# Turning x on TensorE in float32 instead of by the DMA queue, and re-ordering the experts' products and rows, in an attention and two-MoE kernel on one core

## The chip, the core and the metric

The kernel runs on one core of a Trainium2 chip. The core's engines run side by side: TensorE (PE in the profile; PEld is its weight loading), VectorE (DVE), ScalarE (ACT), GpSimd (POOL) and SyncE (SP), which here does nothing but issue DMAs. ACT issues some DMAs as well. Each engine takes its instructions in program order, and waits between engines are semaphores. The metric is the device time of one execution in microseconds, the median of several runs.

## The reference

Three stages follow one another; the output of one is the input of the next.

```python
# attention: batch 4, 8 heads, 576 rows, head size 64
scores = scale * q @ k.T                         # per batch and head
scores = where(scores >= max(scores) - tau, scores, -1e9)
attn = exp(scores - max(scores)); attn /= attn.sum() + 1e-9
x = (attn @ v), heads side by side               # 2304 x 512
# first MoE: one expert, d_ff 2048
h = x @ w_in;  g = maximum(0.01 * h, h);  x = g @ w_out
# second MoE: 8 experts of 4 slots each, hidden 1024
logits = x @ phi                                 # 2304 x 32
slot_input = softmax_over_tokens(logits).T @ x   # 32 x 512
slot_out[e] = maximum(slot_input[e] @ w1[e], 0) @ w2[e]
out = softmax_over_slots(logits) @ slot_out      # 2304 x 512
```

## The kernel before

The 2304 tokens are cut into 18 tiles of 128. Float32 accuracy in the large products is kept by splitting an operand into two 16-bit words, a high one and a low one (`value - high`), and adding three products.

**The order of the work** is not written by hand. `emit` describes operations (`Plan.add`: engine or alternative engines, priority, planned duration, buffers read and written), and `Plan.schedule` places them greedily by planned times; its result is the program order of every engine. So a change of one operation moves others, too. PSUM has few buffers: "S" (2) for the scores, "X" (1) for the attention output, "h" (2) for the first MoE's products, "misc" (1) for all small things.

**One tile in the main loop.** `attention(t)` makes the scores (L1089), the row maximum (DVE L1102), the exponential (ACT L1123), the threshold (DVE L1130), the high word (ACT L1156) and the low words (POOL L1166), turns the probabilities by DMA (SP L1188, two transposing DMAs for a pair of heads) and multiplies with v into X (PE L1198). Then x is X divided by the row sums (DVE L1220), its high word (ACT L1228), its low word (L1231, on DVE or POOL as the plan decides), and a transposing DMA of eight 128x128 blocks into the tile `xT` (SP L1238). `feed(t, xT, xh)` multiplies xT with w_in: 48 matmuls of 512 columns (PE L1266) in four groups j of twelve, each into one "h" buffer, which ACT empties (L1279, L1285); the low word of r (L1288, POOL or DVE) and a transposing DMA (SP L1311) follow, and the logits (PE L1321, L1325). `block` folds two tiles into the running slot sums (PE L1494). Beside the first tiles w_in and w_out are converted from 64-bit words, and w_out is stored to a scratch tensor.

**The tail** comes after the last tile. The slot sums are turned (L1647), multiplied with w_out, which is loaded back (L1659, four accumulating groups c side by side in the four 32-column strips of TensorE), and turned again (L1672). Then come the experts. `load` (L1690) brings in 64 pieces of w1 and 64 of w2, each 256 KB in a buffer of the pool of tags `CH`, as buffers of the main loop come free. The w1 products (L1702) run for expert group G (4 experts), half n of the hidden columns, expert j, and innermost the four pieces k of the contraction; expert j writes strip 32j to 32j+31 of the output. So four matmuls in a row accumulate in one strip:

```python
for j in range(4):
    e = 4 * G + j
    for k in range(4):
        w = load(a["w1"][e, k * P : (k + 1) * P, n * 512 : (n + 1) * 512], T0 - 7)
```

The results are turned (L1715) for the w2 products (L1773), two matmuls of 256 columns for each piece, and the output is made in two halves of 256 columns: one matmul for each tile (L1802), emptied by ACT or DVE (L1809, L1812), stored for two tiles at a time (L1820). A piece of w2 is read, and the output written, as two runs of 256 floats (1 KB) on a partition. Stores of the first half are issued behind the last load.

Of the kernel before, what the change touches and what calls it, by code (L numbers as in the profile page):

```python
# [9 lines left out]
F32 = mybir.dt.float32  # L10
# [10 lines left out]
P = 128  # L21
# [320 lines left out]
def emit(tc, a, out, dbg=None, opt=None):  # L342
# [4 lines left out]
    O = dict(  # L347
        LH=2.3, LB=2.6, HG=3, NR=13, NT=6, NW=5, XH=1, XT=4, KX=10, VX=5, AE=2, AH=3, AT=3, QH=2, QL=2,
        QR=2, TQ=("qr", "raw"), KR=2, VR=4, RAW=1, G=2, PO=0.3, PI=-8.0, PV=-3.0, DA=-100, TK=("kr",
        "w2"), TV=("vr", "kr"), TX=("kx", "w2"), TH=(0, 2), VP=1, MT=0, PS=0.15, NM=6, E=1, LA=2, MG=0,  # L350
        MH=0, RES=0, MI=(2, 1, 2, 1), MO=(1, 1, 1, 1), WT=("w",), PST=0, BH=1, DP={"vr": 1.0, "xT":
        0.1, "xh": 0.25, "X": -0.25, "kx": -1.0, "x32": 0.1, "g": 0.25, "E": -0.1, "S": -1.0, "h": 1.0,
        "r": 1.0, "rT": 0.5, "qr": 1.0, "ql": 0.25, "qh": 1.0, "ah": 0.5, "vx": -0.1, "misc": -1.0,
        "dh": -0.25, "kr": -0.25, "z": -0.1, "th": 0.5, "aT": -1.0}, LO=4, LP=2, PB=1, TU=("x32", "xh",
        "xT", "rT"), TO=("raw", "rT"), TE=18, TR=18, TG=("g",), BI={"spa": 300}, LG=0, CAP=(("aT",
        1),), PL=-0.5, TL=("rT", "xT", "ae"), NA=24, QU=(), CT=0, CX=("aT",), TW=("aT", "ql", "qh",
# [368 lines left out]
    for k in range(4):  # L725
        w32, pk = floats_of(PW, a["w_in"], k, (S23, ("x32", "rT", "xh", "xT"), "raw_in"))
# [410 lines left out]
    def attention(t):  # L1137
# [5 lines left out]
        for pr in range(4):  # L1143
# [40 lines left out]
            for i in range(2):  # L1184
# [571 lines left out]
    HC, firsts = DM // 2, []  # L1756
    outv = out.rearrange("(t i p) d -> t p i d", i=2, p=P)
    so_ps = pl.buf("X", [P, 2, HC])
    for hf in range(2):
        pt = T0 + 2 + hf  # L1760
        cols = slice(hf * HC, hf * HC + HC)
# [34 lines left out]
        for t in range(0, NTILE, 2):  # L1796
# [8 lines left out]
            for i in range(2):  # L1805
# [29 lines left out]
def host(inputs):  # L1835
# [10 lines left out]
    va = np.concatenate([vf, np.concatenate([vl, vl], axis=2)], axis=3)  # L1846

    def bits(w):
        return np.ascontiguousarray(np.asarray(w)).view(np.int64)
# [24 lines left out]
```

## Time and profile before

| | |
|---|---|
| median of 3 runs | 666.04 us (664.19 to 670.23) |
| the profiled execution | 668.88 us, of which 667.1 us are the span of the profile |
| busy share of the span | PE 79%, DVE 66%, ACT 64%, POOL 52% |
| DMA queue of SP | 90.3% of 16 engines' span |
| matrix clock granted, mean | 0.934 |
| instructions | 15257 |

The profile is one execution. Its span starts with the first instruction. Stages can be told by the lines that run in them: conversions until about 115 us, the steady loop until about 537 us, the last tile's products until 566 us, then the tail. [...] Matmul durations overlap each other, so the distance between starts, not the duration, says what a matmul costs. A float32 matmul shows as two records, one for each pass.

### The profile page before, as it was taken

To read this page: it belongs to the slowest core of one execution; us is meant where nothing else is said; L and a number is where in the kernel's file an instruction comes from. 1 tells how busy PE (TensorE), PEld (TensorE's weight loads), DVE (VectorE), ACT (ScalarE), POOL (GpSimd) and SP (SyncE) were. 2 spreads that over 40 slices of the span, in tenths; PEclk is the share of its full clock that TensorE was granted. 3 is DMA by queue.
4 is the path that set the end of the run, shared out by engine and by line. 5 is a ranking of instruction groups with operands and counts; after the bars stand their busy time and mean duration, and the time that the engine had idled before them with its cause. 6 is when DMAs were issued, how large, how long until landed. Compare 5 with 4: busy or idle time off the path is not lost. (4 is left out here: it accounts for less than half of the span.)

```text
span 667.1 us, 15257 instructions
## 1 busy us (share of the span) xinstructions
PE 527.1 (79%) x5622; PEld 322.4 (48%) x5622; DVE 442.1 (66%) x1068; ACT 425.9 (64%) x806; POOL 345.9 (52%) x364
## 2 busy tenths in 40 slices
PE   0111787989799988889799989898979696499994
PEld 0011576666466545555465556565545453132553
DVE  6999978888678767878686976577776531201033
ACT  7999778776587776889677867575765542111022
POOL 3553445575676676868657877676774600000000
PEclk9999967989899999999699999799999897789998
DMA  8954889998999999999989999999998999899995
GB/s 304 338 212 123 201 227 217 249 198 183 168 192 236 190 172 186 178 211 213 182 162 189 189 155 192 207 186 168 171 156 144 256 224 242 283 381 348 365 311 196
DMA packets 316522, 145.26 MB, mean 218 GB/s; under 512 B 270624, under 2 KB 291616, under 8 KB 316448
## 3 DMA queue, kind: packets, MB, share of 16 engines
q1 hardware_dynamic: 309248, 130.56, 90.3%
q10 hardware_dynamic: 7200, 13.73, 8.3%
q8 instruction: 44, 0.72, 0.5%
q14 instruction: 30, 0.25, 0.1%
HBM read 69.27 MB, written 8.91 MB: 117 GB/s over the span
## 5 line engine op out<-in xcount | busy, mean ns | idle before, releaser
L1166 POOL TENSOR_TENSOR ah<-ae,ah 128x512 f16<-128x512 f32 (+1 forms) x216 | 206.4, 978 | 97.4 <-ACT ah L1156 72.2
L1266 PE MATMUL h<-wh,xT 128*128 128x512 f16 x864 | 217.4, 391 | 10.0 <-DMA xT<-xh 9.8
L1102 DVE TENSOR_REDUCE nm<-S 128x1 f32<-128x576 f32 x144 | 103.0, 748 | 62.7 <-PE S L1089 62.7
L1123 ACT ACTIVATE ae<-S,nm 128x576 f32<-128x576 f32 x144 | 100.8, 738 | 40.6 <-DVE nm L1102 32.9
L1266 PEld LDWEIGHTS <-xT 128*128 128x128 f16 x864 | 77.6, 101 | 91.3 <-issue 12.7
L1130 DVE SCALAR_TENSOR_TENSOR ae<-S,th,ae 128x576 f32<-128x576 f32 x144 | 113.7, 812 | 11.1 <-ACT ae L1123 10.3
L1198 PE MATMUL X<-vx,aT 128*128 128x64 f16 (+1 forms) x2240 | 94.2, 200 | 30.0 <-DMA aT<-ah 29.9
L1198 PEld LDWEIGHTS <-aT 128*128 128x128 f16 (+1 forms) x2240 | 82.4, 105 | 62.8 <-DMA aT<-ah 41.7
L1156 ACT ACTIVATE ah<-ae 128x576 f16<-128x576 f32 x144 | 96.0, 681 | 10.5 <-DVE ae L1130 8.9
L1089 PE MATMUL S<-kx,qh 64*128 64x288 f32 (+1 forms) x600 | 82.4, 340 | 6.8 <-DVE ae L1130 6.2
L1279 ACT ACTIVATE g<-h 128x512 f32<-128x512 f32 x72 | 42.9, 596 | 49.5 <-PE h L1266 42.7
L1089 PEld LDWEIGHTS S<-kx,qh 64*128 64x128 f32 (+1 forms) x600 | 56.0, 199 | 25.9 <-issue 21.5
L1288 POOL TENSOR_TENSOR r<-g,r 128x512 f16<-128x512 f32 x42 | 48.8, 1166 | 17.1 <-ACT r L1285 17.1
L1089 PE MATMUL S<-kx,ql 64*128 64x288 f32 (+1 forms) x280 | 48.3, 316 | 11.2 <-DVE ql L975 11.2
L1285 ACT ACTIVATE r<-g 128x512 f16<-128x512 f32 x72 | 45.0, 628 | 0.4
L1288 DVE TENSOR_TENSOR r<-g,r 128x512 f16<-128x512 f32 x30 | 28.9, 965 | 20.1 <-ACT r L1285 20.1
L1089 PEld LDWEIGHTS S<-kx,ql 64*128 64x128 f32 (+1 forms) x280 | 32.3, 202 | 11.6 <-DVE ql L975 11.6
L496 PE MATMUL misc<-c,tmp 128*1 128x128 f32 x16 | 4.5, 380 | 33.4 <-DVE tmp L563 30.0
L1321 PE MATMUL misc<-c,rT 128*128 128x64 f16 x288 | 19.0, 190 | 9.5 <-DMA rT<-r 9.5
L1321 PEld LDWEIGHTS <-rT 128*128 128x128 f16 x288 | 17.5, 97 | 12.2 <-DMA rT<-r 10.0
L799 PE MATMUL misc<-c,w 128*128 128x32 f32 x128 | 19.3, 298 | 4.4 <-DVE w L791 2.6
L1231 POOL TENSOR_TENSOR xh<-x,xh 128x512 f16<-128x512 f32 x12 | 14.4, 1200 | 15.3 <-ACT xh L1228 12.6
(334 smaller groups left out, 828.8 us busy)
## 6 DMA issues: line engine op xcount, KB each, us to landing
wh<-in_w SPq DMA_DIRECT2D x29, 256.0 KB, 6.4
r<-in_w SPq DMA_DIRECT2D x24, 256.0 KB, 5.2
rT<-in_w_out SPq DMA_DIRECT2D x22, 256.0 KB, 3.5
ah<-in_w_in SPq DMA_DIRECT2D x9, 512.0 KB, 5.9
kx<-in_w SPq DMA_DIRECT2D x16, 256.0 KB, 5.9
ae<-in_w_in SPq DMA_DIRECT2D x7, 512.0 KB, 4.3
vr<-in_v SPq DMA_DIRECT2D x10, 320.0 KB, 4.1
scr<-w SPq DMA_DIRECT2D x12, 256.0 KB, 3.9
```

Source lines behind the costliest of these rows:

```text
L1089: pe.matmul(out=pss[i].ap[:rows, n, :HALF], lhsT=l.ap[64 * i : 64 * i + 64, pr, :rows], rhs=m.ap[64 * i : 64 * i + 64, n * HALF : (n + 1) ...
L1102: lambda: dve.tensor_reduce(out=nm.ap, in_=ps.ap[:, :, :HALF], axis=AX.XY, op=ALU.max, negate=True),
L1123: lambda: act.activation(out=e(), in_=ps.ap[:, :, :HALF], func=AF.Exp, bias=nm.ap[:, 0:1], scale=1.0),
L1130: lambda: dve.scalar_tensor_tensor(out=e(), in0=ps.ap[:, :, :HALF], scalar=th.ap[:, 0:1], in1=e(), op0=ALU.is_ge, op1=ALU.mult, accum_out= ...
L1156: (lambda ah, ae, i: lambda: act.activation(out=ah.ap[:, i, :S], in_=ae.ap[:, i], func=AF.Copy))(ah, ae, i),
L1166: (lambda ah, ae: lambda: pool.tensor_tensor(out=ah.ap[:, h, w0 : w0 + c1 - c0], in0=ae.ap[:, h, c0:c1], in1=ah.ap[:, h, c0:c1], op=ALU.su ...
L1198: pe.matmul(out=X.ap[r0:r1, 2 * pr + i], lhsT=aT.ap[:, c, r0:r1], rhs=vtiles[b, pr].ap[:, wv, cv], start=(pr == 0 and i == 0 and n == 0), ...
L1266: pe.matmul(out=hp.ap, lhsT=xT.ap[:, wx * 4 + k], rhs=wh[k][j].ap[:, ww], start=(n == 0), stop=(n == 11),)
L1279: (lambda g, hp: lambda: act.activation(out=g.ap, in_=hp.ap, func=AF.Prelu, alpha=0.01))(g, hp),
L1285: (lambda j, g: lambda: act.activation(out=r[j].ap[:, 0], in_=g.ap, func=AF.Copy))(j, g),
L1288: fg = lambda eng, j, g: lambda: eng.tensor_tensor(out=r[j].ap[:, 1], in0=g.ap, in1=r[j].ap[:, 0], op=ALU.subtract)
L1321: pe.matmul(out=L.ap, lhsT=rT[j].ap[:, c], rhs=wq.ap[:, 4 * j + c], start=(j == 0 and c == 0), stop=False,)
```

## The change

Four things change. (1) x is turned by four float32 transposes on PE (L1229 of the new code) into an "h" buffer of PSUM, out of which ACT writes the high word of `xT` (L1233) and DVE the low word (L1238, always DVE). The ACT copy and the subtraction in front of the DMA, the tile `xh`, and the transposing DMA go. `x32` has two buffers now. (2) The w1 loop has the expert j innermost. (3) The host stores w2 such that a piece is one run of 2 KB on each partition. (4) The output tensor has a layout in which a store writes one run of 2 KB for each partition; the host puts it in order afterwards.

```diff
-        xh, xT = pl.buf("xh", [P, 2, DM], F16), pl.buf("xT", [P, 8, P], F16)
+        xp, xT = pl.buf(O["XP"], [P, 4, P], F32, "xp"), pl.buf("xT", [P, 8, P], F16)
+
+        def f():
+            for k in range(4):
+                pe.transpose(xp.ap[:, k], x32.ap[:, k * P : (k + 1) * P], ident.ap)
+
+        pe_op(p, 440, f, r=[x32, ident], w=[xp])
         act_op(
-            p, t_act(512), lambda: act.activation(out=xh.ap[:, 0], in_=x32.ap, func=AF.Copy),
-            r=[x32], w=[(xh, 0)],
-        )
-        fx = lambda eng: lambda: eng.tensor_tensor(
-            out=xh.ap[:, 1], in0=x32.ap, in1=xh.ap[:, 0], op=ALU.subtract
-        )
-        add_alt(p, [("dve", P2(t_dve(512)), fx(dve)), ("pool", t_pool(512), fx(pool))], r=[x32, (xh, 0)], w=[(xh, 1)])
-        att_last.append(
-            dma_t(
-                p, 8,
-                lambda: sp.dma_start_transpose(out=xT.ap, in_=xh.ap.rearrange("p a b -> p (a b)")),
-                r=[xh], w=[xT],
-            )
+            p, 490, lambda: act.activation(out=xT.ap[:, 0:4], in_=xp.ap, func=AF.Copy), r=[xp],
+            w=[(xT, 0)],
+        )
+        dve_op(
+            p, 602,
+            lambda: dve.tensor_tensor(
+                out=xT.ap[:, 4:8], in0=xp.ap, in1=xT.ap[:, 0:4], op=ALU.subtract
+            ),
+            r=[xp, (xT, 0)], w=[(xT, 1)],
         )
...
-            for j in range(4):
-                e = 4 * G + j
-                for k in range(4):
+            for k in range(4):
+                for j in range(4):
+                    e = 4 * G + j
                     w = load(a["w1"][e, k * P : (k + 1) * P, n * 512 : (n + 1) * 512], T0 - 7)
...
                     w = load(
-                        a["w2"][4 * G + j, c * P : (c + 2) * P, cols].rearrange("(k p) d -> p k d", p=P),
-                        T0 - 7, [P, 2, HC],
+                        a["w2"][hf, 4 * G + j, c // 2].rearrange("p (k d) -> p k d", k=2), T0 - 7, [P, 2, HC]
                     )
...
-                (lambda t, ot, cols: lambda dq: dq.dma_start(
-                    out=outv[t // 2, :, :, cols], in_=ot.ap))(t, ot, cols),
+                (lambda t, ot, hf: lambda dq: dq.dma_start(
+                    out=out[hf, t // 2], in_=ot.ap.rearrange("p i d -> p (i d)")))(t, ot, hf),
```

Lines behind L1073 have other numbers in the new code: 2 less in the attention, 1 more in `feed` and in the tail's w1 part. The next rows are ACT's order around the x of the twelfth tile, before. `x` is the float32 tile, `xh` its two words, `ah` the probabilities' words, `dh` a small tile of `block`.

```order
L1123 ACTIVATE ae<-S,nm 128x576 x2
L1401 ACTIVATE sm<-sm 128x1
L1409 ACTIVATE E,sm<-misc,sm 128x256
L1228 ACTIVATE xh<-x_6282 128x512
L1156 ACTIVATE ah<-ae 128x576
```

And ACT's order at the same tile now; `g` and `r` (L1280, L1286) are the emptying of an "h" buffer of the tile before.

```order
L1121 ACTIVATE ae<-S,nm 128x576 x2
L1280 ACTIVATE g<-h 128x512
L1286 ACTIVATE r<-g 128x512
L1233 ACTIVATE xT<-h 128x512
L1154 ACTIVATE ah<-ae 128x576 x2
```

ACT's part of x stood behind two exponentials and the work of `block`; it now stands behind the emptying of the last product of the tile before, and reads PSUM. The next rows are PE's order at the same place now: the last matmul of the tile before, the four transposes, twelve score matmuls, and the first of fourteen X matmuls of the next tile (L1196); the first matmul that reads the new `xT` follows those fourteen.

```order
L1267 MATMUL h<-wh,xT 128x512
L1229 MATMUL h<-c_78,x_6370 128x128 x4
L1087 MATMUL S<-kx,qh 128x288 x4
L1087 MATMUL S<-kx,ql 128x288 x2
L1087 MATMUL S<-kx,qh 128x288 x4
L1087 MATMUL S<-kx,ql 128x288 x2
L1196 LDWEIGHTS aT
L1196 MATMUL X<-vx,aT 128x64
```

Before, PE had no instruction between X and the first product of a tile that belonged to x. The last piece is DVE's order there now: x (L1218), thresholds, two selections of the next tile's scores (L1128), the low word of `xT`.

```order
L1218 TENSOR_TENSOR x_6370<-X,rz 128x512
L1107 TENSOR_SCALAR th<-nm,c_101 128x1
L1128 SCALAR_TENSOR_TENSOR ae,z<-S,th,ae 128x576 x2
L1238 TENSOR_TENSOR xT<-h,xT 128x512
L1100 TENSOR_REDUCE nm<-S 128x1 x2
```

The low word stood on POOL for 12 of the 18 tiles before; it stands on DVE behind two selections now.

## Rows read from the trace of the kernel before

**Rows 1.** Busy time by stage: stretch, length, engines (instructions), PEclk, DMA share, GB/s

```profile
115.00:537.00 422.00, 373.27 (x4528) 236.08 (x4528) 315.06 (x755) 301.79 (x562) 291.38 (x306) 0.96 1.06 190
...
537.00:566.00 29.00, 24.36 (x158) 10.95 (x158) 8.52 (x17) 10.30 (x22) 0.50 (x1) 0.88 1.07 241
...
588.50:627.40 38.90, 38.59 (x153) 11.96 (x154) 3.50 (x7) 5.14 (x9) 0.00 (x0) 0.96 1.08 362
...
654.50:667.10 12.60, 3.89 (x20) 2.76 (x20) 5.40 (x13) 3.33 (x8) 0.00 (x0) 0.74 0.57 188
```

**Rows 2.** The x transposing DMA (L1238): durations of issue, first and last start, who waited

```profile
L1238 SPq DMA_TRANSPOSE xT<-xh x18: 1231/1252/3459, 112.9 to 541.1; - x18
...
  PE h L1266: 9.8, 6
```

**Rows 3.** Timeline of the twelfth and thirteenth tiles: start, us, engine, line, [idle before]

```profile
387.84 0.68 DVE L1220 TENSOR_TENSOR x<-X,rz 128x512 f32<-128x512 f32 x1
...
391.79 1.23 SPq L1238 DMA_TRANSPOSE xT<-xh  x1
...
395.05 1.47 PE L1266 MATMUL h<-wh,xT 128*128 128x512 f16 x6 [1.02 <-DMA xT<-xh]
...
422.81 1.46 PE L1266 MATMUL h<-wh,xT 128*128 128x512 f16 x3 [3.31 <-DMA xT<-xh]
```

**Rows 4.** Busy time in a stretch behind the longest of these waits

```profile
421.50:428.40 6.90, 5.59 (x30) 3.27 (x30) 2.23 (x4) 1.08 (x3) 4.16 (x5) 0.51 1.19 244
```

**Rows 5.** Groups by line: busy us, mean ns of one, idle before and releaser

```profile
L1198 PE MATMUL X<-vx,aT 128*128 128x64 f16 (+1 forms) x2240 | 94.2, 200 | 30.0 <-DMA aT<-ah 29.9
...
L1231 POOL TENSOR_TENSOR xh<-x,xh 128x512 f16<-128x512 f32 x12 | 14.4, 1200 | 15.3 <-ACT xh L1228 12.6 <-issue 1.8 <-DMA aT<-ah 0.8
...
L789 ACT ACTIVATE w<-h 128x512 f32<-128x512 f32 x9 | 5.4, 598 | 5.6 <-PE h L783 5.6
L791 DVE COPY w<-h 128x512 f32<-128x512 f32 x7 | 4.8, 688 | 3.3 <-PE h L783 3.2
```

**Rows 6.** PE timeline: groups of four float32 transposes, at full and at low clock

```profile
588.81 1.09 PE L1745 MATMUL misc<-c,qr 128*96 128x128 f32 x4 [0.44 <-DVE aT L1679]
...
631.94 0.60 PE L1715 MATMUL h<-c,qh 128*128 128x128 f32 x4
```

**Rows 7.** Chain of waits: the last X matmuls of the last tile; then its products' records

```profile
537.08 0.58 PE X L1198 x14
...
L1266 PE MATMUL h<-wh,xT x864: 376/379/634, 116.3 to 565.8; 128*128 128x512 f16 x173
```

**Rows 8.** PE timeline: w_out products with four strips in turn, then w1 products

```profile
585.39 0.59 PE L1659 MATMUL h<-raw,aT 128*32 128x512 f32 x1
...
585.41 0.59 PE L1659 MATMUL h<-vx,aT 128*32 128x512 f32 x1
585.82 0.59 PE L1659 MATMUL h<-raw,aT 128*32 128x512 f32 x1
...
600.16 0.62 PE L1702 MATMUL S<-xT,aT 128*32 128x512 f32 x1
600.17 0.62 PE L1702 MATMUL S<-x,aT 128*32 128x512 f32 x1
600.61 0.59 PE L1702 MATMUL S<-xT,aT 128*32 128x512 f32 x1
```

**Rows 9.** SP's timeline: issue of the first and of the last w2 load

```profile
593.59 0.38 SPq L1690 DMA_DIRECT2D kr<-in_w  x1
...
640.49 0.37 SPq L1690 DMA_DIRECT2D kr<-in_w  x1
```

**Rows 10.** DMA packets from 577 to 594 us (w1), and from 600 to 620 us (w2)

```profile
DMA packets 3631, 6.64 MB, mean 390 GB/s; under 512 B 404, under 2 KB 404, under 8 KB 3628
...
DMA packets 7213, 6.97 MB, mean 349 GB/s; under 512 B 421, under 2 KB 7212, under 8 KB 7212
```

**Rows 11.** DMA issues: KB each, median us from issue to landing

```profile
r<-in_w SPq DMA_DIRECT2D x24, 256.0 KB, 5.2
```

More of the change, by code (lines that the diff above doesn't have):

```diff
@@ L347, in emit @@
     O = dict(
-        LH=2.3, LB=2.6, HG=3, NR=13, NT=6, NW=5, XH=1, XT=4, KX=10, VX=5, AE=2, AH=3, AT=3, QH=2, QL=2,
+        LH=2.3, LB=2.6, HG=3, NR=13, NT=6, NW=5, NX=2, XT=4, KX=10, VX=5, AE=2, AH=3, AT=3, QH=2, QL=2,
         QR=2, TQ=("qr", "raw"), KR=2, VR=4, RAW=1, G=2, PO=0.3, PI=-8.0, PV=-3.0, DA=-100, TK=("kr",
-        "w2"), TV=("vr", "kr"), TX=("kx", "w2"), TH=(0, 2), VP=1, MT=0, PS=0.15, NM=6, E=1, LA=2, MG=0,
+        "w2"), TV=("vr", "kr"), TX=("kx", "w2"), TH=(0, 2), VP=1, MT=0, PS=0.15, NM=6, E=1, LA=2, XP=("h",), MG=0,
         MH=0, RES=0, MI=(2, 1, 2, 1), MO=(1, 1, 1, 1), WT=("w",), PST=0, BH=1, DP={"vr": 1.0, "xT":
@@ L353, in emit @@
         "r": 1.0, "rT": 0.5, "qr": 1.0, "ql": 0.25, "qh": 1.0, "ah": 0.5, "vx": -0.1, "misc": -1.0,
-        "dh": -0.25, "kr": -0.25, "z": -0.1, "th": 0.5, "aT": -1.0}, LO=4, LP=2, PB=1, TU=("x32", "xh",
-        "xT", "rT"), TO=("raw", "rT"), TE=18, TR=18, TG=("g",), BI={"spa": 300}, LG=0, CAP=(("aT",
+        "dh": -0.25, "kr": -0.25, "z": -0.1, "th": 0.5, "aT": -1.0}, LO=4, LP=2, PB=1, TU=("x32", "xT",
+        "rT"), TO=("raw", "rT"), TE=18, TR=18, TG=("g",), BI={"spa": 300}, LG=0, CAP=(("aT",
         1),), PL=-0.5, TL=("rT", "xT", "ae"), NA=24, QU=(), CT=0, CX=("aT",), TW=("aT", "ql", "qh",
@@ L413, in emit @@
         ("r", "main", O["NR"]), ("rT", "main", O["NT"]), ("w", "main", O["NW"]),
-        ("x32", "main", 1), ("xh", "main", O["XH"]), ("xT", "main", O["XT"]),
+        ("x32", "main", O["NX"]), ("xT", "main", O["XT"]),
         ("qr", "main", O["QR"]), ("qh", "main", O["QH"]), ("ql", "main", O["QL"]), ("kr", "main", O["KR"]),
@@ L568, in floats_of @@
         return ws, pow2_of(prio, hw)
-    pl.early.update(("raw_in", "raw_out"))
+    pl.early.update(("raw_in", "raw_out", "xp"))
     if O["WT"] != ("w",):
@@ L725, in emit @@
     for k in range(4):
-        w32, pk = floats_of(PW, a["w_in"], k, (S23, ("x32", "rT", "xh", "xT"), "raw_in"))
+        w32, pk = floats_of(PW, a["w_in"], k, (S23, ("x32", "rT", "xT"), "raw_in"))
         sk = scale_from(PW + 0.16, pk, 4.0)
@@ L1071, in split_v @@
         vtiles[b, pr] = vx
-    att_last = []
     def scores(t, pr, prio, qs):
@@ L1225, in attention @@
         )
-        xh, xT = pl.buf("xh", [P, 2, DM], F16), pl.buf("xT", [P, 8, P], F16)
+        xp, xT = pl.buf(O["XP"], [P, 4, P], F32, "xp"), pl.buf("xT", [P, 8, P], F16)
[3 more added lines that the diff above has]
+        pe_op(p, 440, f, r=[x32, ident], w=[xp])
         act_op(
-            p, t_act(512), lambda: act.activation(out=xh.ap[:, 0], in_=x32.ap, func=AF.Copy),
-            r=[x32], w=[(xh, 0)],
-        )
-        fx = lambda eng: lambda: eng.tensor_tensor(
-            out=xh.ap[:, 1], in0=x32.ap, in1=xh.ap[:, 0], op=ALU.subtract
-        )
-        add_alt(p, [("dve", P2(t_dve(512)), fx(dve)), ("pool", t_pool(512), fx(pool))], r=[x32, (xh, 0)], w=[(xh, 1)])
-        att_last.append(
-            dma_t(
-                p, 8,
-                lambda: sp.dma_start_transpose(out=xT.ap, in_=xh.ap.rearrange("p a b -> p (a b)")),
-                r=[xh], w=[xT],
-            )
+            p, 490, lambda: act.activation(out=xT.ap[:, 0:4], in_=xp.ap, func=AF.Copy), r=[xp],
+            w=[(xT, 0)],
+        )
+        dve_op(
[4 more added lines that the diff above has]
+            r=[xp, (xT, 0)], w=[(xT, 1)],
         )
         dump(f"x{t}", x32, lambda q: q)
-        return xT, xh
+        return xT, None
     acc, accx = const([P, 512]), const([P, P]) if wlq else None
@@ L1599, in emit @@
     T0 = NTILE + 10.0
-    CH = ("wh", "kx", "kr", "vr", "vx", "qr", "r", "rT", "w", "w2", "raw", "xh", "xT", "x32") + O["CX"]
+    CH = ("wh", "kx", "kr", "vr", "vx", "qr", "r", "rT", "w", "w2", "raw", "xT", "x32") + O["CX"]
     TW = O["TW"]
@@ L1756, in emit @@
     HC, firsts = DM // 2, []
-    outv = out.rearrange("(t i p) d -> t p i d", i=2, p=P)
     so_ps = pl.buf("X", [P, 2, HC])
@@ L1760, in emit @@
         pt = T0 + 2 + hf
-        cols = slice(hf * HC, hf * HC + HC)
         for G in range(2):
@@ L1846, in host @@
     va = np.concatenate([vf, np.concatenate([vl, vl], axis=2)], axis=3)
+    w2 = np.asarray(inputs["moe2_w2"]).reshape(8, 4, 2, P, 2, DM // 2)
+    w2a = w2.transpose(4, 0, 1, 3, 2, 5).reshape(2, 8, 4, P, DM)
     def bits(w):
@@ L1853, in host @@
         "w_out": bits(inputs["moe_w_out"]), "phi": np.asarray(inputs["moe2_phi"]),
-        "w1": np.asarray(inputs["moe2_w1"]), "w2": np.asarray(inputs["moe2_w2"]),
+        "w1": np.asarray(inputs["moe2_w1"]), "w2": w2a,
     }
@@ L1868 @@
     }
-    out = nc.dram_tensor("out", (NT, DM), F32, kind="ExternalOutput").ap()
+    out = nc.dram_tensor("out", (2, NTILE // 2, P, DM), F32, kind="ExternalOutput").ap()
     with tile.TileContext(nc) as tc:
@@ L1872 @@
     r = run_bass_kernel_spmd(nc, [{"in_" + n: x for n, x in arr.items()}], core_ids=[0])
-    return r.results[0]["out"]
+    y = r.results[0]["out"].reshape(2, NTILE // 2, P, 2, DM // 2)
+    return np.ascontiguousarray(y.transpose(1, 3, 2, 0, 4)).reshape(NT, DM)
```

## The prediction

> **What bounds the kernel now.** I read the table of busy times by stage first. In the steady loop from 115 to 537 us PE is busy 373 of 422 us, DVE 315, ACT 302, POOL 291 [rows 1]. PE is the fullest engine at 88%, and the other three, at 69% to 75%, form the ring that feeds it. The x transposes of SP start at 112.9 for the first tile and at 541.1 for the last [rows 2]: 428 us for 17 steps, 25.2 us for a tile. So the loop is neither a clean PE bound nor a clean latency bound: PE has 49 us of idle time in it, and what is put on PE will be paid for most of the way.
>
> The waits come next. PE idled 9.8 us, in 6 waits, for the turned x [rows 2], and 29.9 us for the turned probabilities [rows 5]. In the twelfth tile x starts on DVE at 387.84, SP issues its turn at 391.79, and the product that needs it starts at 395.05, after 1.02 us of idle PE; in the thirteenth the wait is 3.31 us [rows 3]. [...]
>
> The tail is another matter. From 588.5 to 627.4 PE is busy 38.6 of 38.9 us and every other engine nearly nothing [rows 1]. In it the w1 products start in pairs: two experts 0.01 us apart, the next only 0.43 us later [rows 8]. The w_out products just before, whose loop takes four strips in turn, start all four within 0.02 us and the next four 0.43 us later [rows 8]. The DMA side is full as well: 64 loads of w2 take from 593.59 to 640.49 [rows 9], at 349 GB/s in runs of 1 KB, where the w1 loads ahead of them made 390 GB/s in runs of 2 KB [rows 10]. PE is done with w2 at 654.5, the start of the last stage, 14 us after the last issue; a load lands 5.2 us after its issue [rows 11]; so PE lags the data by 8.8 us, and the PE chain, not the loads, ends the tail today. The last stage takes 12.6 us [rows 1].
>
> **The tail, part by part.** *w1 with the expert innermost.* Sixteen matmuls for each of four outputs, 64 in all, two passes each. With four strips in turn a group of four costs 2 x 0.43 us, so 16 groups cost 13.8 us. The stage of 38.9 us holds besides 18 transposes and the first turn of h, together some 3.5 us by the price of 0.6 us for four [rows 6]. So 35 us become 14, and PE would be 21 us earlier. All of that can't be kept: the w2 loads come at the pace of the DMA queue, which was full already, and a buffer that comes free sooner doesn't speed it. What is kept is PE's lag of 8.8 us, less some 2 us that the last matmuls need behind the last landing: -6.8 us.
>
> *Runs of 2 KB.* The 46.9 us of w2 loads shrink by 349/390 to 42.0: -4.9 us. The nine stores at the end, 2.4 MB, which the last stage ends with, take 6.8 us at 349 GB/s and 6.1 at 390: -0.7 us.
>
> [...]
>
> *What is paid.* [...] And the load stream starts against a shorter last tile (below), so fewer pieces are in when the last product ends: +1.5 us. Tail: -6.8 - 4.9 - 0.7 + 1.0 + 1.5 = **-9.9 us**. Bounds: -13 if neither is paid and PE keeps up within 0.5 us, -4 if PE's order makes it lag as before and only the loads gain.
>
> **The main loop, part by part.** *Four transposes on PE for each tile.* A group of four costs 0.60 us at full clock and 1.09 at the low one [rows 6]. 18 x 0.60 = 10.8 us; bounds 0 (all in PE's idle time) and 19.6. PE is busy 88% of the loop, so I charge 88%: +9.5.
>
> *The wait for the DMA goes.* -9.8 us [rows 2], and the half clock behind the longest, 6.9 us at 0.51 [rows 4], gives back 3: -12.8 together. Bound on the small side: none, when another wait ends last at the same places.
>
> *A wait on ACT and DVE comes.* By the order rows the turn is followed by 12 score matmuls and 14 X matmuls, then the first product that reads xT. ACT's copy out of PSUM and DVE's subtraction aren't in the trace; their nearest rows are the copies of an "h" buffer into SBUF, 0.60 us on ACT and 0.69 on DVE [rows 5]. ACT's copy stands behind the emptying of the last product of the tile before (two instructions), DVE's behind two selections. With nothing late the low word is ready about 2.7 us after the turn starts, and PE has some 1.7 us of work in between. So a wait of up to 1 us for each tile; I charge half of it, 18 x 0.5 = +9. Bounds 0 (ACT and DVE run ahead) and 18 x 1.8 = 32 (two busy queues late at every tile).
>
> *POOL, SP and DVE.* POOL loses 12 subtractions of 1.2 us [rows 5], SP 18 issues of 1.25 us [rows 2], both ahead of the turns of the probabilities that PE waits 29.9 us for; I take an eighth: -3.7. DVE gains 18 x 0.69 less the 6 it did before, 8 us on an engine busy 75%: a quarter, +2.
>
> *The last tile.* Its last X matmuls end at 537.7 and its last product starts at 565.8 [rows 7]: 28 us, of which 48 products of 0.22 us need 10.4; before them stand the products of the tile before. In the new order those are done by then (one product is left instead of some forty), so that the stretch is about 14 us. The products aren't gone, they stand in the loop: 8.6 us of work at 88%, 9.8 us. -14.1 + 9.8 = -4.3. "h" has two buffers, and x takes one of them for some 2 us a tile; that is in the wait above.
>
> Loop: +9.5 - 12.8 + 9 - 3.7 + 2 - 4.3 = **-0.3 us**, with -10 and +20 as ends that I believe.
>
> **The sum.** 668.9 (profiled execution: span 667.1 and 1.8 around it) - 9.9 - 0.3 = 658.7. That execution is 2.8 us above the median of the runs shown (668.88 to 666.04), so the forecast for a median is 655.9: **656**.
>
> **The rivals.**
> *The loop gains too.* PE's 49 idle us swallow the turns, ACT and DVE are ahead, and the waits for x stay away: the charge of 9 falls to 2 and that of 9.5 to 5, so 656 - 11 = 645. For it: POOL and SP are freed where PE waits longest. Against: ACT's copy stands behind the emptying.
> *The loop pays in full.* Turns 10.8, waits 1 us a tile: 656 + 9 = 665. For it: PE is the fullest engine.
> *Slower.* One mechanism: PE stands at the first product of each tile, because the low word is behind ACT's emptying and DVE's two selections, each released by scores that PE itself makes later. At 1.8 us a tile it costs 23 us more than charged: 679. It decides from 0.9 us a tile above my 0.5. Against it: the order puts 26 small matmuls in between.
> *2 KB is no better than 1 KB.* Then the loads end where they end now: 656 + 4.9 + 0.7 = 661.6. [...]
>
> **How the numbers follow.** The forecast (650 to 661) 50%, the gaining loop 20%, the paying loop 14%, slower 9%, rows without effect 7%. Of the forecast's 50, 6 lie above 659.4, which is 1% under the median; 1% is about what a measurement of this kernel can tell from no change. Faster: 44 + 20 = 64%. Within 1%: 6 + 14 + 7 = 27%. Slower: 9%. The range of 643 to 668 leaves out the slower case, a part of the gaining and a part of the paying one: 80%.
>
> **What would show it.** Right: no DMA wait at L1267; PE idle there, on DVE, of about 9 us; 64 w1 products in 14 us, after which PE waits for w2 loads; those at about 0.67 us each; x starts 25 us apart as now. Wrong: more than 25 us of idle time at L1267, an "h" wait at the turn, w1 starts still 0.43 us apart in pairs, or w2 loads still at 0.74 us.

## The result, and the profile after

| | before | changed |
|---|---|---|
| median, same chip | 668.13 us (4 runs, 664.19 to 670.52) | 628.52 us (4 runs, 623.89 to 632.77) |
| ratio | | 0.9411, 95% interval 0.9315 to 0.9507 |
| span of the profiled execution | 667.1 us | 623.9 us |
| last product of the main loop (L1266, now L1267) starts | 565.8 us | 533.1 us |
| from there to the end of the span | 101.3 us | 90.8 us |

The change takes 39.6 us off the median; the forecast was 10. The last two lines say where: the tail gave 10.5 us (forecast 9.9), and the main loop gave 32.7 us, for which the forecast had 0.3. Some executions are longer in a slower state (of 19 of the kernel before, beside the four kernels below, nine took 654.35 to 663.33 us and ten 664.54 to 675.02); medians here are over all executions, ratios over the faster ones alone, so the two don't follow from one another exactly.

The table of busy time by stage answers to [rows 1]. The columns are stretch, length, busy time of PE, PEld, DVE, ACT and POOL with instructions, granted clock (PEclk, TensorE's, as a share of the full one), DMA share, GB/s. The first fence is before, from 115 us to the last product of the loop. The second is the changed kernel: the same stretch, the steady loop up to x of the last tile, the last tile's products, and the w1 products.

```profile
115.00:565.80 450.80, 397.44 (x4684) 246.95 (x4685) 323.58 (x772) 312.09 (x582) 291.89 (x307) 0.95 1.06 193
```

```profile
115.00:533.10 418.10, 386.10 (x4725) 242.88 (x4725) 318.68 (x759) 309.91 (x573) 287.07 (x321) 0.99 1.03 194
115.00:518.00 403.00, 373.95 (x4642) 237.00 (x4641) 314.21 (x751) 304.11 (x562) 287.07 (x321) 0.99 1.03 190
518.00:533.10 15.10, 12.15 (x84) 5.89 (x84) 4.46 (x9) 5.80 (x11) 0.00 (x0) 1.00 1.09 291
...
557.50:576.80 19.30, 19.12 (x146) 6.01 (x146) 3.28 (x6) 4.54 (x8) 0.00 (x0) 0.91 1.05 386
```

In the loop PE is busy 93% of the time where it was 88%, at a clock of 0.99 instead of 0.96. The last tile's stretch, from the start of its x to its last product, is 15.4 us instead of 28.1, and the w1 stage 19 instead of 39. From the third tile to the last x starts every 24.1 us, where it was 25.4 (362.2 and 380.5 us for 15 steps). So the 32.7 us are 18.3 in the period, 12.7 in the last tile, and 1.7 ahead of the third tile.

The rows from 115 us to the last product split the same 32.7 us another way. PE's idle time, length less busy time, fell from 53.4 to 32.0 us: 21.4. The other 11.3 are PE's busy time, 397.4 and 386.1 us, although the new transposes add some 10.6 to it. Most of that is the granted clock: at 0.95 over 450.8 us a stretch loses some 22 us of full clock, at 0.99 over 418.1 some 4 (an estimate from these two rows). So there are two gains: less waiting, and PE at its full clock for more of the loop. (Before, the stretch of [rows 4] stands at 0.51, and the one behind it, 428.4 to 434 us, at 1.00.)

The next fence is the groups by line on PE in the loop of the changed kernel, from 115 to 533.3 us; it answers to [rows 2] and [rows 5] (busy us, mean ns | idle time before, and who ended it).

```profile
L1267 PE MATMUL h<-wh,xT 128*128 128x512 f16 x840 | 207.8, 384 | 3.5 <-ACT xT L1233 1.7 <-DVE xT L1238 1.1 <-ACT w L789 0.7
L1196 PE MATMUL X<-vx,aT 128*128 128x64 f16 (+1 forms) x2072 | 81.2, 195 | 18.7 <-DMA aT<-ah 17.6 <-DVE x L1218 0.8
...
L1229 PE MATMUL h<-c,x 128*128 128x128 f32 x68 | 10.6, 279 | 1.6 <-DVE x L1218 1.4 <-DVE th L1107 0.2
```

PE's wait for the x words is 2.8 us in all, where the DMA's was 9.8, and the wait for the turned probabilities has fallen from 29.9 to 18.0 us over the whole span, although nothing of theirs was changed. That second number is the trail.

One caution for all that follows: a stage's length comes from one profile of each kernel. The kernel before and three kernels below (`experts_only`, `w1_only`, `rows_only`) have the same instructions in the same order on PE, DVE and ACT up to that point, and their last products start between 559.3 and 566.6 us. A difference of some 7 us between two profiles is therefore not clear of noise. The last tile's stretch was 28.1 us in the profile before, but 22.1 to 23.2 us in the three others with the old x path, so a part of its 12.7 us belongs to that one profile.

### The profile page after: what moved, and what is told of

The parts are those of the page before. It is cut to its first block, busy times and chain, and to the rows that moved or that the text cites. A ratio compares the mean times of both kernels' runs of the same rounds, so it can differ in the third digit from the quotient of the medians.

```text
span 623.9 us, 15356 instructions
## 1 busy us (share of the span) xinstructions
PE 509.2 (82%) x5694; PEld 318.3 (51%) x5694; DVE 438.0 (70%) x1055; ACT 425.3 (68%) x802; POOL 342.9 (55%) x381
## 4 chain that ended last, share of the span: by engine, by line
PE 42%; DMA 17%; DVE 15%; ACT 11%; POOL 6%; issue 6%; SPq 1%; ACTq 0%; POOLq 0%; DVEq 0%
PE h L1267 14%; DMA aT<-ah 12%; PE S L1087 7%; PE X L1196 6%; PE X L1771 4%; POOL ah L1164 4%; DVE nm L1100 3%; DVE ae L1128 3%; PE S L1703 3%; DMA rT<-r 2%; PE misc L1495 2%; ACT ae L1121 1%; ACT ah L1154 1%; DVE w L640 1%; DMA rT<-in_w_out 1%
## 5 line engine op out<-in xcount | busy, mean ns | idle before, releaser
L1164 POOL TENSOR_TENSOR ah<-ae,ah 128x512 f16<-128x512 f32 (+1 forms) x216 | 203.1, 963 | 92.4 <-ACT ah L1154 71.9
L1267 PE MATMUL h<-wh,xT 128*128 128x512 f16 x864 | 213.8, 384 | 3.5 <-ACT xT L1233 1.7
L1128 DVE SCALAR_TENSOR_TENSOR ae<-S,th,ae 128x576 f32<-128x576 f32 x144 | 114.0, 814 | 9.4 <-ACT ae L1121 8.3
L1267 PEld LDWEIGHTS <-xT 128*128 128x128 f16 x864 | 76.2, 99 | 79.8 <-issue 7.0
L1196 PE MATMUL X<-vx,aT 128*128 128x64 f16 (+1 forms) x2240 | 90.3, 197 | 19.1 <-DMA aT<-ah 18.0
L1196 PEld LDWEIGHTS <-aT 128*128 128x128 f16 (+1 forms) x2240 | 78.6, 103 | 49.8 <-DMA aT<-ah 31.2
L1087 PE MATMUL S<-kx,qh 64*128 64x288 f32 (+1 forms) x620 | 79.8, 328 | 5.2 <-DVE ae L1128 4.9
L1289 POOL TENSOR_TENSOR r<-g,r 128x512 f16<-128x512 f32 x49 | 56.8, 1159 | 19.4 <-ACT r L1286 19.3
L1087 PEld LDWEIGHTS S<-kx,qh 64*128 64x128 f32 (+1 forms) x620 | 54.0, 189 | 24.5 <-issue 16.6
L1280 ACT ACTIVATE g<-h 128x512 f32<-128x512 f32 x72 | 42.7, 593 | 28.7 <-PE h L1267 27.9
L1286 ACT ACTIVATE r<-g 128x512 f16<-128x512 f32 x72 | 45.1, 629 | 1.0
L496 PE MATMUL misc<-c,tmp 128*1 128x128 f32 x16 | 4.3, 364 | 34.3 <-DVE tmp L563 29.8
L1289 DVE TENSOR_TENSOR r<-g,r 128x512 f16<-128x512 f32 x23 | 20.2, 878 | 13.5 <-ACT r L1286 11.6
L1113 POOL TENSOR_SCALAR th<-nm,c 128x1 f32<-128x1 f32 x49 | 14.8, 302 | 22.9 <-DVE nm L1100 14.7
L799 PEld LDWEIGHTS misc<-c,w 128*128 128x128 f32 x128 | 19.5, 226 | 5.3 <-DVE w L791 2.0
```

Of the source, the lines that this page charges most:

```text
L1087: pe.matmul(out=pss[i].ap[:rows, n, :HALF], lhsT=l.ap[64 * i : 64 * i + 64, pr, :rows], rhs=m.ap[64 * i : 64 * i + 64, n * HALF : (n + 1) ...
L1128: lambda: dve.scalar_tensor_tensor(out=e(), in0=ps.ap[:, :, :HALF], scalar=th.ap[:, 0:1], in1=e(), op0=ALU.is_ge, op1=ALU.mult, accum_out= ...
L1164: (lambda ah, ae: lambda: pool.tensor_tensor(out=ah.ap[:, h, w0 : w0 + c1 - c0], in0=ae.ap[:, h, c0:c1], in1=ah.ap[:, h, c0:c1], op=ALU.su ...
L1196: pe.matmul(out=X.ap[r0:r1, 2 * pr + i], lhsT=aT.ap[:, c, r0:r1], rhs=vtiles[b, pr].ap[:, wv, cv], start=(pr == 0 and i == 0 and n == 0), ...
L1267: pe.matmul(out=hp.ap, lhsT=xT.ap[:, wx * 4 + k], rhs=wh[k][j].ap[:, ww], start=(n == 0), stop=(n == 11),)
L1280: (lambda g, hp: lambda: act.activation(out=g.ap, in_=hp.ap, func=AF.Prelu, alpha=0.01))(g, hp),
```

## Experiments: which part gives what

Four kernels take the change apart. `x_only` keeps the old experts' part, `experts_only` the old x path; the other two hold one half of the experts' part each. Code from here on is shortened to the lines that matter.

```diff
 # x_only: the changed kernel with the old order of w1, the old w2 and output layout
-for k in range(4):
-    for j in range(4):
+for j in range(4):
+    for k in range(4):
 # experts_only: the kernel before, with both edits of the experts' part
 # w1_only: the kernel before, with the w1 loop alone
 # rows_only: the kernel before, with the 2 KB runs of w2 and output alone
```

> Only the x part: x turned by TensorE, the tail as before. Theory A, the loop is where the forecast failed (last w_in product 32.7 us earlier in the profile of the changed kernel): 28 to 33 us less than before, about 637. Theory B, the forecast of the loop was right and the loop looks shorter only because the tail's loads no longer press on the queue during it: within 5 us of before.

> Only the experts' part: w1 with the expert innermost, w2 and output in runs of 2 KB; x by the DMA queue as before. Theory A: 8 to 11 us less than before, about 658, as the tail's terms of the forecast said (-9.9). Theory B: 25 us or more less than before.

> Only the w1 loop with the expert innermost. The forecast's term: 6.8 us less, with the w1 products in some 14 to 18 us instead of 36 and TensorE waiting for loads of w2 afterwards. Rival: the w1 products aren't nearer together than now (0.43 us for two) and nothing moves.

> Only the runs of 2 KB for w2 and the output. If TensorE's chain and not the loads ends the tail before, as the forecast says, the loads end some 5 us earlier and the time falls by 0 to 2 us (the stores' 0.7). Rival: the loads end the tail, and the time falls by 5 us or more.

| kernel | median, us | ratio to before, 95% interval | last product of the loop | from there to the end |
|---|---|---|---|---|
| before, beside these four | 664.54 | | 565.8 | 101.3 |
| x_only | 638.02 | 0.9634 (0.9587 to 0.9680) | 537.6 | 101.3 |
| experts_only | 652.67 | 0.9770 (0.9685 to 0.9855) | 566.6 | 89.6 |
| w1_only | 655.91 | 0.9879 (0.9839 to 0.9920) | 564.6 | 93.6 |
| rows_only | 664.88 | 1.0077 (1.0034 to 1.0119) | 559.3 | 102.5 |

The parts add up: by the ratios x alone takes off 3.7% and the experts 2.3%, together 6.0%, and both at once 5.9%. In the last two columns x moves the loop by 28.2 us and the tail not at all; the experts' kernels move the tail, and the loop only within the spread of profiles (`experts_only`'s profile is the longest of its four executions). So the loop's gain is the x part's (theory A), and the tail didn't reach into the loop.

The tail went as its terms said. With the expert innermost the w1 products start over 16.8 us instead of 36.3, and the tail is 7.7 us shorter (forecast 6.8). Its w2 products then start over 38.1 us instead of 26.3, which fits the forecast's PE that waits for loads. The runs of 2 KB alone gain nothing, the ratio is 0.8% on the slow side: SP issues the last load 44.7 us after the first w1 product instead of 50.7, but PE's w2 products take the same 26.3 us as before. Behind a faster PE they may give some 3 to 4 us (93.6 to 89.6 in the profile, 655.9 to 652.7 in the median); the intervals of the two ratios overlap, so that is not shown.

## Experiments: what in the x part

*Theory, short turn.* What counts is that x is turned in 4 us instead of 7. *Theory, order.* What counts is the new plan, in which the products of a tile no longer pile up behind the next. *Theory, queue.* What counts is the transposing DMA that is gone from SP and from the DMA engines. Four runs set these against one another. `ord_dma` has the order of the changed kernel with the DMA's turn:

```diff
-            for k in range(4):
-                pe.transpose(xp.ap[:, k], x32.ap[:, k * P : (k + 1) * P], ident.ap)
+            act.activation(out=xh.ap, in_=x32.ap, func=AF.Copy)
+            sp.dma_start_transpose(out=xT.ap[:, 0:4], in_=xh.ap)
+            dve.tensor_tensor(out=xl, in0=x32.ap, in1=xh.ap, op=ALU.subtract)
+            sp.dma_start_transpose(out=xT.ap[:, 4:8], in_=xl)
```

> The changed kernel with every engine's order of its own, but x turned by the DMA queue again: ACT's and DVE's instruction at the same places make the two words in SBUF, and SP turns each by a DMA of four blocks. Theory order (the new order by itself is what gains, since products of the tile before no longer pile up): within 6 us of the changed kernel, 628 to 634. Theory short turn (the order is good only because the turn is short): in the new order the first product follows x by 1.6 to 5 us, and the DMA path needed 7 us before, so TensorE stands some 3 us at each of 18 tiles: +30 to +55 us, 660 to 685, slower than or like before.

It took 708.44 us, ratio 1.064 (1.0494 to 1.0786). The row of its products from the groups by line, 115 to 545 us:

```profile
L1266 PE MATMUL h<-wh,xT 128*128 128x512 f16 x709 | 194.5, 411 | 46.9 <-DMA xT<-c 24.7 <-DMA xT<-x 22.0
```

So the order gains nothing with this DMA. It puts the first product close behind x, and PE stands 46.9 us there. (Two DMAs of four blocks for each tile instead of one of eight also load SP more than before: some 2.4 us of issue for each tile instead of 1.24, an estimate from the 1.18 us for one block and 1.24 us for eight in `sp_small` and `sp_extra` below. So not all of the 80 us more than the changed kernel is this wait.) `ord_old_pe` is the opposite, the order of before (with the experts' part) and PE's turn, which stands where the plan had the DMA:

```diff
-            sp.dma_start_transpose(out=xT.ap, in_=xh.ap.rearrange("p a b -> p (a b)"))
+            for k in range(4):
+                pe.transpose(xp[:, k], x32.ap[:, k * P : (k + 1) * P], ident.ap)
+            act.activation(out=xT.ap[:, 0:4], in_=xp, func=AF.Copy)
+            dve.tensor_tensor(out=xT.ap[:, 4:8], in0=xp, in1=xT.ap[:, 0:4], op=ALU.subtract)
```

> The kernel with the experts' part alone (653 us), in its own order on every engine, but with x turned by TensorE: four transposes, ACT's copy and DVE's subtraction stand where the plan had the DMA. Theory order: little of the gain, 646 to 653. Theory short turn: the wait for x (8.7 us), the low clock behind it and SP's issues go, so 10 us or more of the 24 are there, 635 to 643.

It took 666.83 us, ratio 1.0034 (0.9973 to 1.0095), where `experts_only` has 0.9770. Both theories missed. First DVE's row from the table of waits, 115 to 570 us (us, times, longest):

```profile
DVE xT L1236 <- ACT xT L1235: 38.7, 18, 3.5
```

Then two of PE's rows from the groups by line, 115 to 545 us:

```profile
L1200 PE MATMUL X<-vx,aT 128*128 128x64 f16 (+1 forms) x2045 | 83.4, 198 | 15.9 <-DMA aT<-ah 15.4
L1091 PE MATMUL S<-kx,qh 64*128 64x288 f32 (+1 forms) x536 | 72.2, 326 | 16.2 <-DVE ae L1132 15.0 <-DVE tmp L508 0.4 <-DVE ls L1340 0.4
```

The wait for the turned probabilities is half of what it is in `experts_only` (35.1 us in the same view), so the queue's relief is there in the old order too. It is eaten by DVE, which stands 38.7 us in front of an ACT copy that the plan didn't place, and by PE, which then stands 15.0 us for DVE. So neither the turn nor the plan gained without the other.

The next run gives the queue's load back: the changed kernel, and per tile a transposing DMA of xT whose output nobody reads.

```diff
             dve.tensor_tensor(out=xT.ap[:, 4:8], in0=xp.ap, in1=xT.ap[:, 0:4], op=ALU.subtract)
+            sp.dma_start_transpose(out=junk, in_=xT.ap.rearrange("p a b -> p (a b)"))
```

> The changed kernel with one transposing DMA of eight blocks more for each tile, issued by SP behind DVE's part of x, out of xT into a buffer that nobody reads: the queue's load of the kernel before comes back without its latency for x. If the shorter wait for the turned probabilities (29.9 to 18.0 us of TensorE's idle time) is SP's relief: 8 to 14 us more, and that wait back at 26 us or more. If it is the order's or POOL's: 0 to 3 us more. The forecast (an eighth of it and of POOL's part): about 2 us more.

It took 655.35 us, ratio 0.9866 (0.9749 to 0.9984), 27 us more than the changed kernel; its last product starts at 562.6 us, 29.5 later and nearly where it was before. PE's row from the groups by line, 115 to 545 us:

```profile
L1196 PE MATMUL X<-vx,aT 128*128 128x64 f16 (+1 forms) x2072 | 82.0, 196 | 31.0 <-DMA aT<-ah 29.8 <-DVE x L1218 0.8
```

The wait is back at 29.8 us, as the expectation for the queue had it, but the time rose by 27 us where 8 to 14 were expected. A DMA that nobody waits for undoes nine tenths of the loop's gain, 29.5 of 32.7 us: theory queue. Where the rest of the 27 us comes from is in the next section. `turn_twice` prices the other side, PE's part, by making each transpose twice.

```diff
-            for k in range(4):
+            for n in range(8):
+                k = n % 4
```

> The changed kernel with each of the four transposes of a tile made twice, everything else and the order alike: 18 more groups of four, 10.6 us of TensorE's time. The forecast's charge (88% of TensorE's busy time is paid): 9.5 us more, 638. Rival, the loop has room on TensorE: 0 to 4 us more. Rival, the turn delays the ring as well: 13 us or more.

It took 640.02 us, ratio 0.9614 (0.9496 to 0.9732); its last product starts 12.2 us later. So 10.6 us of PE cost 12.2 in the profiles and 11.5 in the medians, near the forecast's charge of 9.5; the interval just touches that of the changed kernel, and the difference to 9.5 is not clear of noise.

## Where the queue's price comes from

The trace shows two parts of a DMA, SP's issue and the transfer, and in the loop of before both are nearly full: SP's issues take 81% of it, and the DMA engines' share is 1.06. This is a part of SP's timeline in the twelfth tile of before (start, duration, line, operation, count; a row of two includes the gap between them). From 383.4 to 412.0, 28.6 us, fifteen such issues take 20.8 us:

```profile
386.18 3.76 SPq L1188 DMA_TRANSPOSE aT<-ah  x2
391.79 1.23 SPq L1238 DMA_TRANSPOSE xT<-xh  x1
393.29 2.70 SPq L1188 DMA_TRANSPOSE aT<-ah  x2
```

Over the loop, from 115 to 565.8 us, SP's DMA issues add up to 364.6 of 450.8 us, 81%: 219 transposing ones of 1.57 us on average, and 44 others. (In the changed kernel they are 323.7 of 418.1 us, 77%: the loop became shorter with them, and SP hardly less full.) That SP does not appear in the profile's table of busy times is a property of the table, which leaves out instructions that issue DMAs.

The DMA engines were full as well, a share of 1.06 in [rows 1]. Here are packets in the loop of before, from 430 to 500 us, and in the w2 stage of the changed kernel, from 580 to 606 us:

```profile
DMA packets 42415, 12.06 MB, mean 172 GB/s; under 512 B 41636, under 2 KB 41636, under 8 KB 42404
```

```profile
DMA packets 5491, 10.04 MB, mean 386 GB/s; under 512 B 608, under 2 KB 608, under 8 KB 5488
```

At a busy share of 1.03 and 1.04 the engines moved 172 GB/s with mostly transposing DMAs and 386 with plain loads, less than half of the rate. (SP's pace alone would give near 172, an estimate: 262 KB in an issue of 1.57 us are 167 GB/s; so the 172 need not be the most that the engines can do.)

Two runs try to price the two parts apart: one with a transposing DMA of one block at the same place, one with a plain load of 256 KB.

```diff
+            sp.dma_start_transpose(out=junk[:, 0:1], in_=xT.ap[:, 0:1].rearrange("p a b -> p (a b)"))   # sp_small
+            sp.dma_start(out=junk, in_=a["w1"][0, 0:P, 0:DM])                                           # sp_load
```

> The changed kernel with one transposing DMA of a single 128x128 block more for each tile, at the same place in SP's order where the run before had one of eight blocks (27 us more). Theory DMA engines (the 16 engines, busy share 1.03 to 1.06 in the steady loop, are what ends the loop, and 262 KB of packets under 512 bytes cost 1.5 us of them all): an eighth of that, 2 to 6 us more, 631 to 634. Theory issue (SP's issue of 1.25 us in front of the next turns is what costs): as much as for eight blocks if the issue takes as long, 18 us more or over.

> The changed kernel with one plain load of 256 KB more for each tile, 2 KB on each partition, at the same place of SP's order, into a buffer that nobody reads. Theory DMA engines: the tail's loads made 390 GB/s, so 0.67 us for each, 18 x 0.67 = 12 us more, 640. Theory transposes only (only transposing transfers hold up the turns of the probabilities): 0 to 4 us more. [...]

The issues of the added DMA in `sp_extra`, `sp_small` and `sp_load` (count, then minimum, median and maximum in ns, first and last start):

```profile
L1239 SPq DMA_TRANSPOSE x<-xT x18: 1231/1242/1979, 105.4 to 550.0; - x18
```

```profile
L1239 SPq DMA_TRANSPOSE x<-xT x18: 1120/1184/2067, 104.4 to 536.6; - x18
```

```profile
L1239 SPq DMA_DIRECT2D x<-in_w x18: 328/574/1542, 104.2 to 530.3; - x18
```

| added for each tile | issue, median | median of the kernel, ratio (95% interval) | loop longer by | for one |
|---|---|---|---|---|
| transposing DMA, 8 blocks | 1.24 us | 655.35, 0.9866 (0.9749 to 0.9984) | 29.5 us | 1.64 us |
| transposing DMA, 1 block | 1.18 us | 643.39, 0.9647 (0.9561 to 0.9734) | 16.0 us | 0.89 us |
| plain load, 256 KB | 0.57 us | 637.59, 0.9566 (0.9491 to 0.9642) | 10.6 us | 0.59 us |

Neither theory is right alone. One block has nearly the issue of eight and an eighth of the transfer, and costs 54% as much: by a straight line through the two, 0.78 us of the 1.64 is there whatever the size, and 0.86 us goes with the eight blocks. The table of busy times by stage shows what these prices consist of, for `sp_extra` and then `sp_small`, from 115 us to the last product:

```profile
115.00:562.60 447.60, 399.47 (x4752) 251.35 (x4749) 323.41 (x760) 312.24 (x578) 289.28 (x323) 0.96 1.03 191
```

```profile
115.00:549.10 434.10, 389.84 (x4751) 245.87 (x4748) 322.20 (x763) 312.36 (x579) 289.95 (x323) 0.98 1.02 189
```

Against the changed kernel's 32.0 us of idle PE and 386.1 of busy PE, eight blocks cost 16.1 us of idle time and 13.4 of busy time; one block costs 12.3 and 3.7. So one block brings back most of the waits, and what eight cost more is mainly that PE does its work at a clock of 0.96 instead of 0.98. The straight line therefore does not separate issue from transfer. A third cost is in it as well: SP stands in front of the added DMA until DVE's word is written, from the end of its issue before, 10.6 us in all in `sp_extra`, 5.3 in `sp_small` and 1.3 in `sp_load`, whose load waits for no word. And the plain load's price of 0.59 us is near both its issue, 0.57 us, and its 256 KB at 390 GB/s, 0.67 us, so that it can't tell the two apart either; its interval just touches that of the changed kernel. What is shown is the price of a DMA in this queue; how it splits is open.

## What ends the loop now

`rt_skip` takes 18 more transposing DMAs out: the fourth rT tile isn't turned, and the logits read the third instead, so a part of the computation is left out. `rt_act` leaves the transfer and moves its issue to ACT. `pool_extra` gives POOL a subtraction more for each tile.

```diff
-            sp.dma_start_transpose(out=rT[j].ap, ...)
+            j < 3 and sp.dma_start_transpose(out=rT[j].ap, ...)        # rt_skip; logits: rT[min(j, 2)]
+            (act if j == 3 else sp).dma_start_transpose(out=rT[j].ap, ...)   # rt_act
+            pool.tensor_tensor(out=junk.ap, in0=ident..., in1=xT.ap[:, 0:4], op=ALU.subtract)  # pool_extra
```

> The changed kernel without the transposing DMA of the fourth rT tile of each 128 tokens; the logits read the third instead, so that part of the computation is left out. Every order is kept but for SP's 18 missing issues. Theory, SP and the queue still end the loop behind the change: as much as 18 of them cost the other way, 20 to 29 us less, 600 to 608. Rival, TensorE ends it now (idle 32 of 418 us): 3 to 12 us less, 616 to 625.

> The changed kernel with the transposing DMA of the fourth rT tile issued by ACT, not by SP, at the place where the plan issues it; the computation is whole. SP loses 18 issues, the 16 DMA engines lose nothing, ACT gains 18 x 1.3 us. If SP's issue is half of the price of a transposing DMA (one block 0.85 us, eight 1.6): 14 us less, and ACT's part gives 0 to 20 of it back: 614 to 634. Rival, the DMA engines alone: not less than now, 628 to 645.

> The changed kernel with one subtraction of 128x512 more on POOL for each tile, at DVE's part of x, into a buffer that nobody reads: what POOL did for x in 12 of 18 tiles before. The forecast's eighth of 1.2 us: 18 x 0.15 = 3 us more. Rival, POOL's low words feed SP's turns and are late as often as SP: 10 to 20 us more.

`rt_skip` took 622.82 us, ratio 0.929 (0.9225 to 0.9355); its loop is 7.0 us shorter, 0.39 for one DMA; the interval overlaps that of the changed kernel. A DMA that costs 1.64 us when added is worth about a quarter of that when one like it is taken away. That fits a bend at the changed kernel: more load on the queue makes SP and the DMA engines the bound, less leaves it to PE, whose idle time in its loop is only 32 of 418 us. The two runs add and take away DMAs at different places, and 7 us is within the spread of profiles, so the bend is argued rather than shown.

`pool_extra` took 633.7 us, ratio 0.9516 (0.9437 to 0.9595); its loop is 7.4 us longer. The interval overlaps that of the changed kernel, and 7.4 us is within the spread of profiles, so this price is not clear of noise: 0.41 us for a subtraction of 1.2. (The expectation speaks of the forecast's eighth of 1.2 us; the forecast's eighth was one of PE's wait of 29.9 us.)

`rt_act` took 699.28 us, ratio 1.0472 (1.0404 to 1.0539), outside both expectations. ACT's rows in the view of that line, waiting for a semaphore and issuing:

```profile
L1312 ACTq EVENT_SEMAPHORE  x57: 17/38/5316, 189.0 to 609.2; - x57
...
L1312 ACTq DMA_TRANSPOSE rT<-r x18: 1248/1256/1519, 191.6 to 609.2; - x18
```

The issue itself is 1.26 us, but ACT also stands in front of it until the low word of r is there, up to 5.3 us, and the next tiles' exponentials stand behind it; PE then waits 31.9 us for rT, where it waited 1.5. The run says nothing on the split between issue and transfer; here the issue was better placed on the engine that does nothing else, with 628.52 us against 699.28.

Two more runs tried to go on in the direction of the change: the last, or the second and the last, of the four rT tiles turned by PE.

```diff
+                for n in range(8):
+                    pe.transpose(rp.ap[:, n], r[j].ap[:, n // 4, n % 4 * P : n % 4 * P + P], id16.ap)
+                act.activation(out=rT[j].ap, in_=rp.ap, func=AF.Copy)   # or DVE, as the plan decides
```

> A further step in the direction of the change: of the four rT tiles of each 128 tokens the last one is turned by TensorE as well (eight transposes of 16-bit words into an h buffer, one copy of 128x1024 by ACT or DVE), not by the DMA queue. Theory DMA engines: 18 transposing DMAs less at 1.5 to 1.6 us, -28; 18 x 0.5 us more on TensorE at its full price, +9 to +11; the copies of about 1 us on ACT and DVE, busy 74%, 0 to +9: between 610 and 622. Rival, the chain of TensorE, DVE and ACT ends the loop now: 628 to 640.

> The same for two of the four rT tiles. Theory DMA engines: less gain than from the first, since TensorE was busy 93% of the loop: 605 to 625. Rival: TensorE and the h buffers end the loop, slower than with one, 625 to 645.

They took 699.39 us, ratio 1.0476 (1.0384 to 1.0569), and 691.01 us, ratio 1.034 (1.0246 to 1.0434). In the first, the row of PE's new transposes (groups by line, 115 to 590 us):

```profile
L1319 PE MATMUL h<-c,r 128*128 128x128 f16 x128 | 12.8, 235 | 16.1 <-ACT r L1290 9.4 <-POOL r L1293 4.8 <-DVE r L1293 2.0
```

The DMA share fell to 0.84 (115 to 533 us), so the queue was relieved; but PE stands 16.1 us for r, which is ready late, and the whole plan came out anew, with a clock of 0.91 in the same stretch and 43.7 us instead of 15.4 for the last tile. How much of the 71 us is the new plan and how much the wait can't be told from these two. No version that does the whole computation and beats the changed kernel was found.

## Why the prediction was wrong, step by step

The step that failed is one term in the main loop, the -3.7 under "POOL, SP and DVE". In its place the runs show -29.5 us for the 18 DMAs alone (`sp_extra`). The forecast took an eighth of the 29.9 us that PE waits for the turned probabilities, so that it priced the queue by one wait that it could see, and not by the queue's own load. The row was there: a DMA share of 1.06 over 422 us [rows 1]. The text read PE as the fullest engine, since the table of busy times lists PE at 88% and SP not at all; in the tail the same text did take a full queue as the bound. Near half of the price, 13.4 of 29.5 us, is not waiting but PE's work at a lower clock, for which the forecast had 3 us, and only behind the wait for x. By step:

| step of the loop | forecast, us | measured | from |
|---|---|---|---|
| transposes on PE | +9.5 | +12.2 | `turn_twice` |
| wait for the DMA, and its low clock | -12.8 | the wait of 9.8 us is gone | PE's row at L1267 |
| new wait for ACT and DVE | +9 | +2.8 | the same row |
| SP and the queue | -3.7, with POOL | -29.5 | `sp_extra` |
| POOL | in the term above | 12 x 0.41 = -4.9, within the spread | `pool_extra` |
| DVE | +2 | not tried | |
| products moved into the loop | +9.8 | not tried | |
| last tile's stretch | -14.1 | -12.7 | 28.1 and 15.4 us |

Up to x of the last tile the forecast was the sum of all but the last line, +13.8, and x starts 20.0 us earlier (537.7 and 517.7). With the measured terms in place of its own the sum is 12.2 - 12.8 + 2.8 - 29.5 - 4.9 + 2 + 9.8 = -20.4. The prices were taken by adding to the changed kernel, one at a time, each from one profile against another, three of the seven terms are the forecast's own, and the 3 us for the low clock may be in the queue's price as well. That they add up this well is luck; only the queue's term is far larger than the spread.

The new wait was the second miss, and small: the products stand behind enough work. In the changed kernel's twelfth tile x starts on DVE at 376.79, PE turns it at 377.62, ACT and DVE write the words, and the next products start on PE at 380.65 without idle time:

```profile
376.79 0.68 DVE L1218 TENSOR_TENSOR x<-X,rz 128x512 f32<-128x512 f32 x1
...
377.62 0.63 PE L1229 MATMUL h<-c,x 128*128 128x128 f32 x4
...
378.90 0.58 ACT L1233 ACTIVATE xT<-h 128x512 f16<-128x512 f32 x1
379.51 0.69 DVE L1238 TENSOR_TENSOR xT<-h,xT 128x512 f16<-128x512 f32 x1 [0.38 <-ACT xT L1233]
```

That is 3.9 us from x to product, where [rows 3] have 7.2. The rival "the loop gains too" had the right sign but gave the gain to PE's idle time, not to the queue, and stopped at 645.

What was right: no DMA wait at L1267; the last tile at 15.4 us (forecast 14; its gain of 12.7 owes something to the profile before, see above); w1 in 18 us (14, at a clock of 0.91 in its stage); w2 loads at 43.6 / 64 = 0.68 us each (0.67); the tail at -10.5 (-9.9). The w2 loads in runs of 2 KB made 386 GB/s where those of 1 KB had 349 [rows 10]; that `rows_only` gained nothing was PE's chain, as the forecast of the tail had it. The 1.0 us for PE's clock in the tail's sum is shown by no run: in the changed kernel the w2 products, from 576.3 to 611.0 us, had a mean clock of 1.00; behind them it was 0.68 (611.0 to 623.9 us) against 0.74, but from the first product there to the end of the span it is 11.7 us, from 612.23, where before it is 12.2, from 654.87. "x starts 25 us apart as now" was wrong by 1.2 us a tile, and "PE idle there, on DVE, of about 9 us" by 6. The paying rival's own sum gives 666, not 665, which changes nothing.

What stays open: how the price of a DMA in the queue divides between SP's issue, SP's standing in front of it, the transfer and PE's clock; and what DVE's part is worth.

## What to carry to other kernels

Before calling an engine the bound, add up the queue that issues DMAs, by the durations of its issues, and look at the DMA share: neither is in the list of busy engines. Don't price a transfer by who waits for it alone: here PE had waited 9.8 us for the x words, and 18 DMAs that nobody reads made the loop 29.5 us longer (`sp_extra`), a price that one run measures. Look at PE's busy time and clock as well as at its waits: here near half of the price was there, 13.4 us. And where a planner sets the order, test a shorter path with its own plan; here neither gained alone (ratios 1.064 for `ord_dma`, 1.0034 for `ord_old_pe`).

## What was not expected of the hardware

The issue of the added transposing DMA hardly changed with its size, 1.18 us for one block (`sp_small`) and 1.24 for eight (`sp_extra`), while a plain load of as many bytes as the eight took 0.57 (`sp_load`; medians). So a transposing DMA of one block was a bad trade here: an eighth of the bytes for 54% of the price, 0.89 us against 1.64. In the changed kernel a read of 128x512 float32 from PSUM with 16-bit output took ACT 0.59 us and DVE 0.69, the forecast's 0.60 and 0.69, and the group of four float32 transposes 0.63 us at full clock, against 0.60 in [rows 6].
